# One tile and one move for queries and keys, the gate by tanh, and a new table of priorities in a three-part sequence mixer

## The chip, the cores and the metric

The kernel runs on one core of a Trainium2 chip. The metric is the time of one execution on the device in microseconds (us). Five engines work at the same time, each through its own queue and strictly in the order in which the program was written: TensorE (PE; its weight loads are shown as PEld), VectorE (DVE), ScalarE (ACT), GpSimd (POOL) and SyncE (SP), which here only issues DMA transfers. An engine that reaches an instruction whose inputs aren't there waits, and everything behind it in its queue waits too.

## What is computed

Four sequences of 768 steps with 8 heads of 48 channels (384 channels together) go through three parts.

```python
# 1. a linear recurrence per head, with complex decay
a = (a_re, a_im) * min(|a|, 0.999) / (|a| + 1e-6)
for t in range(S):
    S_re, S_im = a_re*S_re - a_im*S_im + outer(k[t], v[t]), a_re*S_im + a_im*S_re
    y[t] = q[t] @ S_re
x = y.reshape(B, S, 384)
# 2. a gate from a causal convolution of five taps
gate = 1 / (1 + exp(-conv(x, conv_w)));   x = (gate * (x @ w_val)) @ w_out
# 3. mixing over tokens
theta = x @ w_theta
u = x + w_tok_r @ (x * cos(theta)) + w_tok_i @ (x * sin(theta))
return u + max(u @ w_ch, 0)
```

## The kernel before

Each sequence is worked on in two halves of 384 steps, so there are eight halves `h`; channels lie on the 128 partitions in three blocks `m`. The stages of one half, by the names that the planner gives them:

- `pre_load`, `pre_a`, `pre_e`, `pre_u`, `pre_p` (function `half`): load decay, queries, keys and values; the logarithm of the decay's size and its running sum by a scan (ACT: Ln, Exp; DVE: products and scans), the running angle (ACT: Arctan, then Sin and Cos), and the products that turn `q` and `k` into four tiles, `qc`, `q` and `kc`, `k` (cosine and sine part of each). A square of the imaginary part (line 596) is always ACT's. The tiles `e`, `L`, `cc`, `kc`, `qc` are five allocations from one pool `xx` of three buffers.
- `pre_k`: transposes of `kc` and `k` on TensorE (line 679), copied into `ks`. `pre_m` (line 698): moves of the four tiles from channel layout into head layout, `KT` and `QT`, one pair of heads at a time. A head of 48 channels is one or two pieces of partitions, ten pieces for eight heads; four sources make 40 DMAs per half, 320 in all, from SP's queue.
- `att_s`, `att_q`, `att_x`, `att_m`: the running state, scores (line 746), their mask on DVE (line 750), the output, and its move back to channel layout `xT` (line 789).
- `gat_x`, `gat_c`, `gat_s`, `gat_v`, `gat_p` (function `gated`): split into two half-precision parts, the convolution (TensorE for the first two halves, DVE after, line 842), the gate by `Sigmoid` (lines 830 and 848), the value product times the gate, and the projection with its cosine and sine (lines 902 and 904).
- `mix_y`, `mix_o`, per sequence: the mixing over tokens (line 933, the largest group of matmuls), then the last product (line 964) and the store.
- `w_val`, `w_out`, `w_tok`, `w_ch`: loading and splitting the weights, 37 loads (line 434), taken up by DVE and ACT mostly in the first 250 us.

All of this is first recorded as steps and then put in order by `Plan.order`, a list scheduler: of the steps that are ready it takes the one of lowest score, where a score is a priority by stage and half (`TUNE["aim"]`), a slope within the stage, a price for an engine slower than the fastest that could do it (`slow`), and a price for a change of ACT's function table (`switch`). A step may have alternatives: a copy out of PSUM goes to ACT or DVE. ACT holds one set of functions at a time; a step that names its sets (`table=`) makes `emit` put a table load (line 225) ahead of it when the current set is none of them. Before, `Ln` and `Exp` are one set, `Sigmoid` and `Arctan` can share a second, `Sin` and `Arctan` a third. Flags of the values' ranges are collected in `flag` and summed at the end (line 1009); if one fails, a slow general path runs, which takes no part here.

Of the kernel before, what the change touches and what calls it, by code (L numbers as in the profile page):

```python
# [21 lines left out]
NC = 3  # L22
# [38 lines left out]
class Lazy:  # L61
# [15 lines left out]
class Plan:  # L77
# [37 lines left out]
    def touch(self, st, t):  # L115
        if t not in st.tiles:
            st.tiles.append(t)
            self.claim(t)
# [113 lines left out]
def STAGE(i):  # L232
# [5 lines left out]
    slow=7.561879865749755e+17, switch=6.288666508159823e+19,  # L238
    aim=dict(
        att_m=(2.6995250415312483e+20, -7.969025655037973e+20, 2.6228837826230804e+19, 2.6900520492997217e+20, -8.834881158532012e+18, -2.879741646661289e+20, -5.6941031593171996e+20, 2.3047449587628616e+18),  # L240
        att_q=(-3.098021878434935e+20, -1.1402659875657051e+20, 1.887862893900206e+20, -2.8577290015113812e+20, -1.4315973604769672e+20, 2.6812851596232865e+20, 2.72275845311613e+20, 7.860040540285524e+20),
        att_s=(-8.1055449031404e+20, -7.491206287610686e+20, 2.9358157753418138e+19, -3.8325095700157596e+20, -6.619979384008357e+20, -2.234011386790889e+20, -5.975838226088282e+20, 1.6686986873077983e+20),
        att_x=(1.1113433647480439e+19, -5.647427977795909e+20, -2.8460971411064858e+20, 5.586815476186121e+19, 1.2318998677514333e+20, 3.819798462611895e+20, 2.275797624242207e+20, 3.855677298476604e+20),
        gat_c=(-1.3939695215960621e+20, 8.573466356105659e+20, 2.2571713871496027e+20, 3.3867600113954475e+20, 5.5553098301983103e+20, 3.7001570014350914e+20, 2.5679529280869446e+20, 3.9509943083354974e+20),
        gat_p=(1.1079553435472739e+20, -5.8677250143246785e+20, -3.039805067631806e+20, 1.3995532506697353e+20, 1.4368282293569442e+19, -4.8003306508215596e+20, -5.888518038921008e+19, 3.3768391232254136e+20),
        gat_s=(-1.859713821331812e+20, -1.4068539620445092e+20, 1.2272979418679604e+20, 1.0910490888272282e+20, 1.975120382740974e+20, 2.7909999301427043e+20, -2.5984925365397773e+20, 3.503112540032319e+20),
        gat_v=(-8.243593242166855e+19, -4.8478023647103314e+20, 2.6272218123939388e+20, 7.870475005876767e+20, -2.922333136132161e+20, 2.180085968308735e+20, 8.681066273223144e+19, 6.446000807147153e+19),
        gat_x=(-3.817467868176136e+19, -5.5407993524252e+20, -2.3538641088770815e+20, -5.286011864109842e+19, 1.2214160515683628e+20, -4.3994221524293557e+20, -1.2611788232525521e+20, -8.341909703175887e+20),
        mix_o=(-2.8734628221397905e+19, -1.5117821435577077e+20, 5.5180557681850335e+19, -3.0992713400204735e+20, 8.898697985755559e+19, 1.7189691487411024e+19, 6.015575849622989e+19, 4.689053187148435e+20),
        mix_y=(1.8267901924410455e+20, 4.718088521769894e+18, 2.6659420514735283e+20, 3.8919266864908095e+20, 3.004006273230587e+20, 1.2053661079841625e+21, 2.7156940596173242e+20, 8.425222082850524e+20),  # L250
        pre_a=(-2.1563070898003165e+20, -1.3407216796584958e+20, 6.598887458043333e+20, 4.288137829766081e+20, 2.7732396744020797e+20, 3.7528707274748146e+20, 4.205374047444239e+20, -5.4573270371167496e+20),
        pre_e=(-7.88945782665487e+19, -2.41133541333048e+20, 3.56175050953755e+20, -2.2958653295810013e+20, 2.0580757847809894e+20, -4.06329427432926e+20, 1.4426176750414936e+19, 3.7503300425471115e+19),
        pre_k=(-3.8194358638246057e+18, -4.690711155477919e+20, -1.05651341434556e+20, -3.8497518485941315e+20, 4.801003520091643e+18, 8.729949699788487e+19, 3.3221443421105107e+19, 8.525573064665427e+19),
        pre_load=(1.3647208663803196e+20, 1.7155210766295656e+20, 3.2799160663234006e+20, 3.643770839616477e+20, -8.83912647730307e+20, 1.0804960952804722e+20, 5.5648036868185824e+20, 1.1333686388887786e+20),
        pre_m=(-1.0319521449344616e+20, 1.8639307935649297e+20, -1.96775082810374e+20, 2.582688938750491e+20, 5.142607771115187e+20, 2.687818958364026e+19, -3.5416465535944786e+20, 1.7837533526089567e+20),
        pre_p=(-1.3761746888669947e+20, 6.39581395858005e+20, 7.44612787205641e+20, 1.3673500528991615e+20, 1.579699019194403e+20, 3.6993958742260076e+20, -2.1781512347217582e+20, 3.930708276628839e+20),
        pre_u=(-5.860711647029067e+19, -3.402301592630338e+20, 1.7263712425624768e+20, 3.0143430377465636e+20, -7.724555404449633e+20, 2.7932201631581952e+20, -8.401409740176993e+19, 1.536761573530841e+18),
        w_ch=(9.679107120691147e+18, -8.567667523970695e+19, 9.84845351623264e+19, 2.0631282111325136e+20, 1.2792621986728021e+20, 1.2299703092890036e+20, 8.444280747653703e+19, 9.810840497961917e+19),
        w_out=(2.4173937984678797e+19, 1.8189247227344226e+19, 6.998474788081834e+19, 1.80638580129783e+20, 1.0592462196430992e+20, 1.0269092211592351e+20, 5.455113029523955e+19, 6.902520285647893e+19),
        w_tok=(-2.4274300307598315e+20, 8.890738857751473e+19, -6.164473229195098e+20, 4.051552711302278e+20, -1.5994422517121417e+20, 1.8111768451654405e+20, 1.133253904891538e+20, 9.650836120777289e+19),  # L260
        w_val=(1.885596508505931e+20, -5.177513586728041e+19, 1.3298879856064614e+18, 1.1360663686930627e+20, 2.738565137956907e+19, 2.9941767965625594e+19, 6.726488094765722e+18, -1.1531895753208386e+19)),
# [56 lines left out]
def fast_path(ctx: ExitStack, tc: tile.TileContext, ri, qk, v, w_val, conv_w, w_out, w_theta, w_tok, w_ch, out, count):  # L318
# [234 lines left out]
    def half(h):  # L553
# [6 lines left out]
        def both(ms):  # L560
# [6 lines left out]
            def put(alts, reads, writes, table=None, flag=()):  # L567
# [3 lines left out]
                for t in (*reads, *writes):  # L571
                    if isinstance(t, Lazy):
                        plan.touch(st, t)
# [700 lines left out]
```

## Time and profile before

| | us |
|---|---|
| median of three runs (552.32 to 554.35) | 553.67 |
| the profiled execution | 553.85 |
| its span, first to last instruction | 552.1 |
| TensorE busy in the span | 463.4 |
| VectorE busy | 451.6 |
| ScalarE busy, of it 54 table loads | 350.9, of it 69.3 |

The span is 1.75 us shorter than the execution's own time. A busy share is a mean over stages with different limits, so the table alone tells of no stage what holds it. TensorE's matmuls overlap and their ends are modelled; its busy time is no statement on its rate.

### The profile page before, as it was taken

To read this page: it belongs to the slowest core of one execution; us is meant where nothing else is said; L and a number is where in the kernel's file an instruction comes from. 1 tells how busy PE (TensorE), PEld (TensorE's weight loads), DVE (VectorE), ACT (ScalarE), POOL (GpSimd) and SP (SyncE) were. 2 spreads that over 40 slices of the span, in tenths; PEclk is the share of its full clock that TensorE was granted. 3 is DMA by queue.
4 is the path that set the end of the run, shared out by engine and by line. 5 is a ranking of instruction groups with operands and counts; after the bars stand their busy time and mean duration, and the time that the engine had idled before them with its cause. 6 is when DMAs were issued, how large, how long until landed. Compare 5 with 4: busy or idle time off the path is not lost.

```text
span 552.1 us, 10792 instructions
## 1 busy us (share of the span) xinstructions
PE 463.4 (84%) x4111; PEld 314.3 (57%) x4111; DVE 451.6 (82%) x792; ACT 350.9 (64%) x565; POOL 8.2 (1%) x32
## 2 busy tenths in 40 slices
PE   0026859868996779899999989999999999999993
PEld 0016646646674456666667666677677766655661
DVE  3799999799979898999999997999987573784222
ACT  6998968877948668886988786679563112521000
POOL 0000001000000000000000000000000000000000
PEclk9997976999997889999999999999999999999997
DMA  8847375654447445753125364242122200000001
GB/s 286 311 144 240 117 241 129 203 159 141 149 135 215 117 118 151 218 182 117 44 77 187 86 197 149 78 131 76 47 77 75 70 25 30 15 14 1 30 28 35
DMA packets 39563, 66.87 MB, mean 121 GB/s; under 512 B 8272, under 2 KB 31312, under 8 KB 39504
## 3 DMA queue, kind: packets, MB, share of 16 engines
q1 hardware_dynamic: 39504, 66.11, 38.9%
q8 instruction: 34, 0.56, 0.5%
q14 instruction: 25, 0.20, 0.1%
HBM read 37.76 MB, written 4.72 MB: 77 GB/s over the span
## 4 chain that ended last, share of the span: by engine, by line
PE 42%; DVE 22%; ACT 16%; DMA 10%; SPq 6%; issue 3%; DVEq 0%; ACTq 0%
PE mm L933 17%; PE mm L884 7%; SPq L698 5%; PE mm L964 5%; ACT L225 3%; DMA zt<-in_w_tok_dram 3%; PE sc L746 3%; PE mm L858 3%; PE x L763 3%; DMA xT<-xs 2%; DVE ri L645 2%; PE x L768 2%; DVE at L750 2%; DVE ri L365 2%; DVE g L842 2%
## 5 line engine op out<-in xcount | busy, mean ns | idle before, releaser
L933 PE MATMUL mm<-zz,wt_sb 128*128 128x384 f16 x864 | 147.0, 326 | 0.0
L933 PEld LDWEIGHTS <-wt_sb 128*128 128x128 f16 x864 | 84.3, 98 | 53.1 <-issue 0.6
L884 PE MATMUL mm<-wo_sb,gHL 128*128 128x384 f16 x432 | 79.3, 338 | 4.1 <-DVE zt L365 4.1
L225 ACT ACT_TABLE_LOAD x54 | 69.3, 1283 | 1.7 <-PEq L1261 0.8
L884 PEld LDWEIGHTS <-gHL 128*128 128x128 f16 x432 | 42.9, 101 | 33.3 <-issue 9.2
L746 PE MATMUL sc<-QT,KT 96*128 96x128 f32 x384 | 54.2, 291 | 6.1 <-DMA QT<-q 3.8
L746 PEld LDWEIGHTS sc<-QT,KT 96*128 96x128 f32 x384 | 50.4, 204 | 10.5 <-issue 3.3
L356 ACT ACTIVATE uHL<-tr 128x384 f16<-128x384 f32 x18 | 8.8, 486 | 63.9 <-PE tr L949 63.9
L679 PE MATMUL tr<-ident,xx 128*128 128x128 f32 x72 | 14.8, 315 | 40.6 <-DVE xx L362 34.8
L763 PE MATMUL x<-at,v 128*64 128x128 f32 x384 | 40.9, 289 | 8.1 <-DVE at L750 7.3
L858 PE MATMUL mm<-xHL,wv_sb 128*128 128x384 f16 x216 | 38.4, 326 | 3.4 <-ACT g L830 1.2
L842 DVE SCALAR_TENSOR_TENSOR g<-xT,cw_sb,g 128x384 f32<-128x384 f32 x72 | 40.9, 610 | 0.1
L964 PE MATMUL mm<-wc_sb,uHL 128*128 128x384 f16 x216 | 39.4, 326 | 1.8 <-ACT uHL L356 1.2
L763 PEld LDWEIGHTS x<-at,v 128*64 128x64 f32 x384 | 26.1, 140 | 16.8 <-issue 7.4
L768 PE MATMUL x<-QT,ws 96*48 96x128 f32 x320 | 35.4, 284 | 0.0
L679 PEld LDWEIGHTS tr<-ident,xx 128*128 128x128 f32 x72 | 9.2, 155 | 45.3 <-issue 29.8
L750 DVE TENSOR_TENSOR at<-sc,tri 128x384 f32<-128x384 f32 x64 | 33.7, 551 | 0.2
L858 PEld LDWEIGHTS <-wv_sb 128*128 128x128 f16 x216 | 20.7, 98 | 17.1 <-issue 4.7
L964 PEld LDWEIGHTS <-uHL 128*128 128x128 f16 x216 | 20.5, 98 | 16.4 <-ACT uHL L356 1.6
L365 DVE SCALAR_TENSOR_TENSOR u<-x,mm 128x384 f32<-128x384 f32 x24 | 13.2, 549 | 17.5 <-PE mm L933 17.3
L362 DVE TENSOR_TENSOR zt<-zt,x 128x768 f32<-128x768 f32 x24 | 22.9, 954 | 4.2 <-ACT zt L904 3.1
L365 DVE SCALAR_TENSOR_TENSOR r<-mm,u 128x384 f32<-128x384 f32 x24 | 13.2, 552 | 13.6 <-PE mm L964 13.3
(155 smaller groups left out, 831.1 us busy)
## 6 DMA issues: line engine op xcount, KB each, us to landing
ri<-in_ri_dram SPq DMA_DIRECT2D x14, 576.0 KB, 4.6
zt<-in_w_tok_dram SPq DMA_DIRECT2D x20, 384.0 KB, 3.8
v<-in_v_dram SPq DMA_DIRECT2D x8, 576.0 KB, 5.9
out_dram<-r SPq DMA_DIRECT2D x24, 192.0 KB, 2.0
q<-in_qk_dram SPq DMA_DIRECT2D x7, 576.0 KB, 5.7
k<-in_qk_dram SPq DMA_DIRECT2D x7, 576.0 KB, 5.6
KT<-xx SPq DMA_DIRECT2D x48, 72.0 KB, 2.2
KT<-k SPq DMA_DIRECT2D x48, 72.0 KB, 2.2
```

The lines of the kernel that those rows point to most:

```text
L225: load_table(table)
L365: return [dve(n, lambda: V.scalar_tensor_tensor(out=out(), in0=a(), scalar=scalar, in1=b(), op0=op0, op1=op1, **kw))]
L698: nc.sync.dma_start(out=o()[cs * D + d0:cs * D + d0 + n, i, :], in_=src()[p0:p0 + n, m, :])
L746: T.matmul(out=ps()[:, c, :], lhsT=kT()[:, i, cs], rhs=qT()[:, i, cs], start=(c == 0), stop=(c == NC - 1), skip_group_check=True)
L750: add([dve(HALF, lambda ps=ps, at=at: V.tensor_tensor(out=at(), in0=ps(), in1=tri.unsqueeze(1).to_broadcast([P, NC, P]), op=ALU.mult))], r ...
L763: T.matmul(out=x()[64 * i:64 * i + 64, cs], lhsT=vt()[:, c, hh * D:hh * D + 64], rhs=ats[i]()[:, c, :], start=(c == 0), stop=(c == NC - 1 ...
L768: T.matmul(out=x()[64 * i:64 * i + D, cs], lhsT=ws[c]()[:, hh * D:(hh + 1) * D], rhs=qT()[:, i, cs], start=False, stop=(c == NC - 1), skip ...
L842: add([dve(HALF, lambda m=m, t=t: V.scalar_tensor_tensor(out=g()[:, m], in0=xT()[:, m, t:t + HALF], scalar=cw_sb[:, m, t:t + 1], in1=g()[: ...
L858: T.matmul(out=ps(), lhsT=wv_sb[:, kk, a, m * P:(m + 1) * P], rhs=xHL()[:, b, kk, 4:], start=(kk == 0 and i == 0), stop=(kk == NK - 1 and ...
L884: T.matmul(out=ps(), lhsT=gT()[:, a, kk, c * P:(c + 1) * P], rhs=wo_sb[:, kk, j, b], start=(kk == 0 and i == 0), stop=(kk == NK - 1 and i ...
L933: T.matmul(out=y(), lhsT=wt_sb[:, j, r, a, s * P:(s + 1) * P], rhs=zz_t[b, s]()[:, e, r], start=(s == 0 and r == 0 and i == 0), stop=(s == ...
L964: T.matmul(out=pv(), lhsT=uHL()[:, a, kk], rhs=wc_sb[:, kk, e], start=(kk == 0 and i == 0), stop=(kk == NK - 1 and i == 2))
```

## The change

- The queries and keys of a half are loaded into one tile `qk`, and `e`/`cc`/`qc` and `L`/`kc` share the two parts of one tile `xx` (class `Part` names one part). One DMA then moves both the query's and the key's piece of a head, into one tile `QK`: 20 DMAs of twice the bytes per half in place of 40. A move now names both parts as its inputs. `xx` has two double buffers in place of three single ones, `qk` two double ones in place of two and two, `x2` six in place of seven.
- The gate is computed as tanh of half the argument; the product with the values becomes (gate + 1) times value, and the factor one half goes into the next scale. `Tanh` is asked for in a set that also holds `Sin`. Sets: `Sin` of the gate in the same set as `Tanh`, `Arctan` first in the set that holds `Sin`. A maximum over every eighth gate value goes into eight new flags per partition.
- The square of `pre_a` may go to DVE as well.
- The value tile's padding lies at its end alone, and its load has a stage of its own (`pre_v`).
- The whole table `TUNE` has other numbers; the prices `slow` and `switch` stand in another ratio to the priorities.

```diff
-SET_SIG = ("sigmoid_and_others",)
-SET_SIN = ("trig_and_small",)
-SET_ATAN = ("sigmoid_and_others", "trig_and_small")
+SET_TANH = ("silu_and_others", "sigmoid_and_others")
+SET_SIN = ("trig_and_small", "silu_and_others")
+SET_SIN2 = ("silu_and_others", "trig_and_small")
+SET_ATAN = ("trig_and_small", "sigmoid_and_others")
...
+class Part:
+    def __init__(self, whole, i):
+        self.whole, self.i = whole, i
+    def __call__(self):
+        return self.whole()[:, self.i]
...
-    slow=7.561879865749755e+17, switch=6.288666508159823e+19,
+    slow=5.041324337085933e+27, switch=1.2587493578880431e+20,
...
-        re, im, q, k = (lazy(t, [P, NK, HALF]) for t in ("ri", "ri", "q", "k"))
-        e, L, cc, kc, qc = (lazy("xx", [P, NK, HALF]) for _ in range(5))
+        re, im = (lazy("ri", [P, NK, HALF]) for _ in range(2))
+        qk_t, xx = lazy("qk", [P, 2, NK, HALF]), lazy("xx", [P, 2, NK, HALF])
+        q, k = Part(qk_t, 0), Part(qk_t, 1)
+        e = cc = qc = Part(xx, 0)
+        L = kc = Part(xx, 1)
...
-            put([act(n, lambda x=im_, y=e_: A.activation(out=y(), in_=x(), func=AF.Square))], [im], [e])
+            put([act(n, lambda x=im_, y=e_: A.activation(out=y(), in_=x(), func=AF.Square)),
+                 dve(n, lambda x=im_, y=e_: V.tensor_tensor(out=y(), in0=x(), in1=x(), op=ALU.mult))], [im], [e])
...
-            for nm, dst_t, parts in (("KT", KT_t, (kc, k)), ("QT", QT_t, (qc, q))):
-                                nc.sync.dma_start(out=o()[cs * D + d0:cs * D + d0 + n, i, :], in_=src()[p0:p0 + n, m, :])
+                for cs, (src, pair) in enumerate(((xx, (qc, kc)), (qk_t, (q, k)))):
+                            nc.sync.dma_start(out=o()[cs * D + d0:cs * D + d0 + n, :, i, :], in_=src()[p0:p0 + n, :, m, :])
+                        add([dma(8 * n * HALF, move, True)], reads=[(t, m) for t in pair], writes=[(o, i, cs, d0)])
...
-            add([act(n3, lambda: A.activation(out=g(), in_=g(), func=AF.Sigmoid))], reads=[g] + gm, writes=gm,
-                table=SET_SIG)
+            add([act(n3, lambda: A.activation(out=g(), in_=g(), func=AF.Tanh, scale=0.5))], reads=[g] + gm, writes=gm,
+                table=SET_TANH)
+        add([("dve", 150.0, lambda: V.tensor_reduce(column(F_GATE + h), g()[:, 0, ::8], axis=AX.X, op=ALU.max))],
+            reads=[(g, 0)], writes=[("flag", F_GATE + h)])
...
-            add(tt(ALU.mult, HALF, lambda m=m: g()[:, m], ps, lambda m=m: g()[:, m]), reads=[ps, (g, m)],
+            add(stt(HALF, lambda m=m: g()[:, m], lambda m=m: g()[:, m], 1.0, ps, ALU.add, ALU.mult), reads=[ps, (g, m)],
```

Three places in the built order show what moves. A row is one instruction, or several alike in a row; a tile's name is followed by what it is made from.

SP's queue, before, from the first moves of the second half (`KT` and `QT` from `xx`, `k` and `q`) on, with a load of token weights (L434) among them:

```order
L698 DMA KT<-xx 48x384 x2
L698 DMA KT<-xx 32x384
L698 DMA KT<-xx 16x384
L698 DMA KT<-k 48x384 x2
L698 DMA QT<-xx 48x384
L434 DMA zt<-in_w_tok_dram 128x768
L698 DMA QT<-xx 48x384
L698 DMA QT<-q 48x384 x2
L698 DMA KT<-k 32x384
L698 DMA KT<-k 16x384
L698 DMA KT<-xx 48x384
L698 DMA KT<-k 48x384
```

Six more rows of such moves follow there before the next load. SP's queue, after, at the same place (L807 is the move back to `xT`, L448 the load of token weights):

```order
L716 DMA QK<-xx 48x2x384 x2
L716 DMA QK<-xx 32x2x384
L716 DMA QK<-xx 16x2x384
L716 DMA QK<-xx 48x2x384
L807 DMA xT<-xs 48x384 x2
L716 DMA QK<-qk 48x2x384 x2
L716 DMA QK<-qk 32x2x384
L716 DMA QK<-qk 16x2x384
L716 DMA QK<-qk 48x2x384
L448 DMA zt<-in_w_tok_dram 128x768
```

The same two pairs of heads now take ten moves in place of twenty, and the next load of weights stands behind ten of them.

ACT's queue, before, at the program's start (the first half, by blocks of channels; L596 is the square):

```order
L591 ACTIVATE ri<-ri 128x384
L593 ACTIVATE xx,flag<-ri 128x384
L596 ACTIVATE xx<-ri 128x384
L598 ACTIVATE xx,flag<-xx,one 128x384
L601 ACTIVATE xx<-ri,lneps 128x384
L591 ACTIVATE ri<-ri 128x384
```

ACT's queue, after, at the same place (L609 and L611 are the Ln and Exp, L617 the second Ln):

```order
L609 ACTIVATE ri<-ri 128x384
L611 ACTIVATE xx,flag<-ri 128x384
L609 ACTIVATE ri<-ri 128x384
L611 ACTIVATE xx,flag<-ri 128x384
L617 ACTIVATE xx,flag<-xx,one 128x384 x2
L620 ACTIVATE xx<-ri,lneps 128x384
```

The square has left ACT's queue; DVE has it there (L615, `xx<-ri`), and two blocks go through each step before the next.

ACT's queue, before, where the sine of one half (L902, L904) meets the gate of the next (L848):

```order
L225 ACT_TABLE_LOAD
L902 ACTIVATE zt<-zt 128x384
L904 ACTIVATE zt<-zt,halfpi 128x384
L225 ACT_TABLE_LOAD
L848 ACTIVATE g<-g 128x1152
L356 ACTIVATE uHL<-tr 128x384
L225 ACT_TABLE_LOAD
L902 ACTIVATE zt<-zt 128x384
L904 ACTIVATE zt<-zt,halfpi 128x384
```

ACT's queue, after, where the same two meet (L924, L926 the sine, L866 the gate):

```order
L926 ACTIVATE zt<-zt,halfpi 128x384
L680 ACTIVATE xx<-xx,halfpi 128x1152
L370 ACTIVATE ws<-w 96x384
L370 ACTIVATE zz<-zt 128x768
L916 ACTIVATE zt<-mm 128x384
L866 ACTIVATE g<-g 128x1152
L370 ACTIVATE x_2862<-mm 128x384
L370 ACTIVATE uHL<-tr 128x384
L922 ACTIVATE zt<-zt 128x384
L924 ACTIVATE zt<-zt 128x384
```

No load stands between the gate and the sines around it. The built order of the fast path holds 39 table loads in place of 54, and 349 DMAs in place of 509.

## Rows read from the trace of the kernel before

**Rows 1.** Busy us of each engine (instructions) in five stretches; granted clock, DMA.

```profile
core 0: us, PE busy (x) PEld busy (x) DVE busy (x) ACT busy (x) POOL busy (x), PEclk, DMA share, GB/s
0.00:28.00 28.00, 0.00 (x0) 0.00 (x0) 16.71 (x39) 22.97 (x45) 2.35 (x12) 1.00 0.83 299
28.00:84.00 56.00, 32.85 (x326) 24.90 (x326) 56.00 (x113) 48.06 (x99) 0.30 (x2) 0.86 0.60 185
84.00:224.00 140.00, 117.56 (x1119) 81.27 (x1119) 124.74 (x208) 108.35 (x167) 3.31 (x9) 0.91 0.51 151
224.00:540.00 316.00, 310.04 (x2656) 206.81 (x2653) 250.90 (x422) 170.99 (x256) 2.19 (x10) 1.00 0.28 84
540.00:552.10 12.10, 2.93 (x18) 1.35 (x16) 3.21 (x14) 0.49 (x1) 0.00 (x0) 0.75 0.12 40
```

**Rows 2.** The chain that ended last, shares of the span by engine.

```profile
PE 42%; DVE 22%; ACT 16%; DMA 10%; SPq 6%; issue 3%; DVEq 0%; ACTq 0%
```

**Rows 3.** DVE's waits from 84 to 224 us: for whom, us, times, longest.

```profile
DVE zt L439 <- DMA zt<-in_w_tok_dram: 4.2, 2, 3.7
DVE x L358 <- PE mm L884: 1.6, 2, 0.9
DVE ri L608 <- ACT xx L601: 1.6, 1, 1.6
DVE zt L439 <- DMA zt<-in_w_ch_dram: 1.2, 1, 1.2
DVE g L362 <- ACT g L848: 1.0, 1, 1.0
...
DVE wt_sb L365 <- ACT wt_sb L407: 0.2, 1, 0.2
```

**Rows 4.** DVE's waits in the first 28 us, the longest.

```profile
DVE ri L362 <- ACT xx L593: 5.0, 3, 3.4
```

**Rows 5.** DMA issues of line 698 on SP: duration ns least/median/most, first and last start.

```profile
L698 SPq DMA_DIRECT2D QT<-q x80: 503/589/1750, 34.7 to 432.0; - x80
```

**Rows 6.** SP's timeline, 79 to 97 us: start, us, what.

```profile
79.72 2.41 SPq L698 DMA_DIRECT2D KT<-xx  x4
...
94.36 1.15 SPq L581 DMA_DIRECT2D ri<-in_ri_dram  x1
95.62 0.84 SPq L434 DMA_DIRECT2D zt<-in_w_tok_dram  x2
```

**Rows 7.** DMA issues: count, size, median us from issue to landing.

```profile
out_dram<-r SPq DMA_DIRECT2D x24, 192.0 KB, 2.0
...
KT<-xx SPq DMA_DIRECT2D x48, 72.0 KB, 2.2
```

**Rows 8.** ACT's timeline around a table load: start, us, what.

```profile
96.02 1.16 ACT L606 ACTIVATE ri<-ri 128x1152 f32<-128x1152 f32 x1
97.20 1.28 ACT L225 ACT_TABLE_LOAD   x1
98.50 0.49 ACT L830 ACTIVATE g<-mm 128x384 f32<-128x384 f32 x1
```

**Rows 9.** Groups by line and shape: busy us, mean ns, idle before.

```profile
L225 ACT ACT_TABLE_LOAD x54 | 69.3, 1283 | 1.7 <-PEq L1261 0.8
...
L362 DVE TENSOR_TENSOR ri<-ri,xx 128x1152 f32<-128x1152 f32 x7 | 9.5, 1352 | 0.0
...
L660 ACT ACTIVATE ri<-ri 128x1152 f32<-128x1152 f32 x7 | 8.1, 1158 | 0.0
...
L848 ACT ACTIVATE g<-g 128x1152 f32<-128x1152 f32 x6 | 7.0, 1163 | 2.8 <-DVE g L842 2.7
...
L398 DVE TENSOR_REDUCE flag<-gHL 128x1 f32<-128x48 f16 x4 | 0.9, 223 | 0.0
```

**Rows 10.** DVE's timeline, back to back work: start, us, what.

```profile
93.27 0.55 DVE L365 SCALAR_TENSOR_TENSOR zt<-zt 128x384 int32<-128x384 int32 x1
93.73 0.54 DVE L365 SCALAR_TENSOR_TENSOR wt_sb<-zt,wt_sb 128x384 f16<-128x384 f32 x1
```

More of the change, by code (lines that the diff above doesn't have):

```diff
@@ L115, in touch @@
     def touch(self, st, t):
+        t = t.whole if isinstance(t, Part) else t
         if t not in st.tiles:
@@ L302 @@
         pre_a=0.0,
-        pre_e=0.0,
-        pre_u=6145.339050871748))
+        pre_e=13729.237869499897,
+        pre_u=2123.5850288312477))
 def segments(h):
@@ L568, in put @@
                 plan.sub = ms[0]
-                st = add(alts, reads=[x for t in reads for x in (names(t) if isinstance(t, Lazy) else [t])],
+                st = add(alts, reads=[x for t in reads for x in (names(t) if isinstance(t, (Lazy, Part)) else [t])],
                          writes=[x for t in writes for x in names(t)] + list(flag), table=table)
                 for t in (*reads, *writes):
-                    if isinstance(t, Lazy):
+                    if isinstance(t, (Lazy, Part)):
                         plan.touch(st, t)
@@ L727, in state @@
                     for at in range(0, 2 * D, 32):
-                        T.matmul(out=w()[at:at + 32, o], lhsT=rows[:, at:at + 32], rhs=vt()[:, c, o],
+                        T.matmul(out=w()[at:at + 32, o], lhsT=rows[:, at:at + 32], rhs=vt()[:, c * CH + hh * D:c * CH + (hh + 1) * D],
                                  start=(ti == 0 and hh == 0), stop=(hh == H - 1), skip_group_check=True)
@@ L745, in score @@
                     cs = slice(c * P, (c + 1) * P)
-                    T.matmul(out=ps()[:, c, :], lhsT=kT()[:, i, cs], rhs=qT()[:, i, cs], start=(c == 0),
+                    T.matmul(out=ps()[:, c, :], lhsT=qk_()[:, 1, i, cs], rhs=qk_()[:, 0, i, cs], start=(c == 0),
                              stop=(c == NC - 1), skip_group_check=True)
-            add([pe(654, score, 0.75)], reads=[qT, kT] + parts(qT) + parts(kT), writes=[ps])
+            add([pe(654, score, 0.75)], reads=[qk_] + parts(qk_), writes=[ps])
             add([dve(HALF, lambda ps=ps, at=at: V.tensor_tensor(
@@ L762, in attend @@
                     hh = 2 * p + i
-                    T.matmul(out=x()[64 * i:64 * i + 64, cs], lhsT=vt()[:, c, hh * D:hh * D + 64], rhs=ats[i]()[:, c, :],
+                    T.matmul(out=x()[64 * i:64 * i + 64, cs], lhsT=vt()[:, c * CH + hh * D:c * CH + hh * D + 64], rhs=ats[i]()[:, c, :],
                              start=(c == 0), stop=(c == NC - 1 and ws[c] is None), skip_group_check=True)
@@ L767, in attend @@
                         hh = 2 * p + i
-                        T.matmul(out=x()[64 * i:64 * i + D, cs], lhsT=ws[c]()[:, hh * D:(hh + 1) * D], rhs=qT()[:, i, cs],
+                        T.matmul(out=x()[64 * i:64 * i + D, cs], lhsT=ws[c]()[:, hh * D:(hh + 1) * D], rhs=qk_()[:, 0, i, cs],
                                  start=False, stop=(c == NC - 1), skip_group_check=True)
@@ L772, in heads @@
         add([pe(128 * 2 * (3 + n_ws), attend, 0.77)],
-            reads=ats + [vt, (vt, "pad"), qT] + parts(qT) + [w for w in ws if w is not None], writes=[x])
+            reads=ats + [vt, (vt, "pad"), qk_] + parts(qk_) + [w for w in ws if w is not None], writes=[x])
         add(copy(HALF, lambda: xs()[:64 + D], lambda: x()[:64 + D]), reads=[x], writes=[xs])
@@ L829, in gated @@
             plan.touch(plan.steps[-1], g)
-            add([act(HALF, lambda m=m, ps=ps: A.activation(out=g()[:, m], in_=ps(), func=AF.Sigmoid, scale=1.0 / (SX * SW)), psum=True)],
-                reads=[ps], writes=[(g, m)], table=SET_SIG)
+            add([act(HALF, lambda m=m, ps=ps: A.activation(out=g()[:, m], in_=ps(), func=AF.Tanh, scale=0.5 / (SX * SW)), psum=True)],
+                reads=[ps], writes=[(g, m)], table=SET_TANH)
             plan.touch(plan.steps[-1], g)
```

160 lines of the change are left out of this document (82 added, 78 removed).

## The prediction

> **What bounds the kernel now.** I read the stretches first [rows 1]. From 224 to 540 us TensorE is busy for 310.0 of 316 us at a granted clock of 1.00: there the end is set by TensorE's work and by nothing else. Before that it isn't: TensorE starts late and is busy for 32.9 of 56 and 117.6 of 140 us. In those stretches DVE is the fullest engine: 56.0 of 56 us, then 124.7 of 140. So the kernel runs behind DVE until TensorE has work enough, and behind TensorE from then on. What sets the time is how early DVE has released TensorE's work, and how long DVE stood still on the way: 28 - 16.7 = 11.3 us in the first 28, none to 84, 140 - 124.7 = 15.3 us to 224.
>
> The chain of waits [rows 2] gives TensorE 42%, DVE 22%, ACT 16%, DMA 10% and SP's issuing 6%. ACT and SP aren't full, but they stand between two pieces of DVE's work. DVE's waits from 84 to 224 us [rows 3] show where: two kinds of wait for a load of weights (4.2 and 1.2, together 5.4 us), eleven rows of waits for ACT, from 1.6 down to 0.2, together 6.9 us, and three for TensorE (the first 1.6).
>
> For the order I used one measure: at a matmul, the DVE work that the order puts ahead of what this matmul needs, plus TensorE's work from it to the end. No time can be below that sum. I took each instruction at its row's median time to the engine's next start, because the recorded ends overlap: 0.46 us between two starts where the record says 0.55 [rows 10]; for TensorE at the lower quartile, its full-clock pace. Over all rows that makes 441 us of DVE, 350 of ACT, 429 of TensorE. Before, the highest sum is 307.3 + 197.9 = 505.2 us, in the attention of the sixth half, and the sums are over 500 from the fourth half on. ACT's lead at the start adds to it: there ACT's rows ahead of DVE's exceed DVE's own by 6.6 us, which makes 511.8. With DVE's other idle time ahead of 224 us (4.7 + 15.3), TensorE's 6.0 idle us from 224 to 540 and the 12.1 - 2.9 = 9.2 at the end [rows 1] that is 547.0 of the span's 552.1; 5.1 us stay unplaced. So the measure is close enough to read a change by.
>
> **The change, part by part.** *Order and moved work.* The built order has 15 ACT loads less (15 x 1.283 = 19.2 us [rows 9]); in exchange more copies out of PSUM stand on ACT, so ACT sums to 336 us, 14 less, and DVE to 438, 3 less. In the last figure are squares that DVE takes over (two of 1.35 us [rows 9] and three small ones) and the eight new maxima (8 x 0.22 = 1.8 us [rows 9]). The highest DVE sum is now 259.3 + 248.9 = 508.2 us, at the first mixing product of the second sequence, 3.0 above before. But the start is better balanced: with the squares gone from ACT its lead is 2.3 us in place of 6.6, and both together make 510.5 against 511.8. Term: **-1.3 us**, from +3.0 (if the start doesn't matter) to -4.3.
>
> *The merged moves.* 320 issues of 0.589 us [rows 5] are 188 us of SP's queue; 160 go, so 94 us at the same price. A move has twice the runs, and if its issue cost twice, nothing would be saved; issues of 16, 32 and 48 partitions lie in the same narrow median, so I take the same price. Landing: 72 KB take 2.2 us, 192 KB 2.0 [rows 7], so 144 KB cost nothing more; the scores behind them don't wait longer. What the issues cost before is visible once: from 79.72 us SP issues moves until 94, and only then, at 95.62, the next two loads of weights [rows 6]; DVE's longest wait for a load, 3.7 us, is for one of them [rows 3]. In the new order ten moves stand at that place, not twenty. Of the 5.4 us I take half: **-2.7**, from 0 (the load waits for its buffer, not for the queue) to -5.4. A merged move waits for query and key both; behind it in SP's queue stand moves to `xT` and loads of weights, for which TensorE's gate and DVE would wait. The key's product is the earlier one and the scores need both, so I count that at zero; its price, if a load is held by one more product of 1.35 us [rows 9], is in the slower rival.
>
> *Table loads.* Ahead of that mixing product there stand 28 loads in place of 37. Nine of 37 are a quarter, so I take a quarter of DVE's 6.9 us behind ACT: **-1.7**, from 0 to -6.9. After 224 us the rest of ACT's saving is hidden by TensorE. The row prices a switch at the load alone: 97.20 + 1.28 = 98.48, and the next activation starts at 98.50; the one before ended at 97.18 [rows 8]. The Trainium skill, page "ScalarE: Activation LUTs", section "What ACT_TABLE_LOAD costs", gives the same 1283 ns but adds a drain of about 1380, 2.66 us for a switch. By that the 15 loads would be 39.9 us, an estimate, this term would double and the time would be 545.7; the trace shows no such gap.
>
> *Start.* The first half's value load, 576 KB or 1.9 us at 299 GB/s [rows 1], stood between the loads of the first and second block and now stands behind all. DVE's waits there are 5.0 us in three, of which 3.4 is the first landing [rows 4]; the other 1.6 can shrink. **-0.8**, from 0 to -1.6.
>
> *At zero.* Tanh for Sigmoid: functions of one shape take the same time (1163 and 1158 ns [rows 9]). The added one in the gate's product rides in an instruction of the same shape. Six `x2` in place of seven: the six `zz` are held by the same steps and stay six, so they cover it; without that cover a projection would wait for the mixing of the sequence before. Two double `xx`: the new order lets the third half's first stage begin after 79 us of DVE's work, before after 89, so they hold nothing back there. One more comparison of flags at the end, **+0.2**, bounded by the small reduction's 0.22 [rows 9].
>
> Sum: -1.3 - 2.7 - 1.7 - 0.8 + 0.2 = -6.3. The profiled execution took 553.85 us and lies 0.2 above the median; against the median, 553.7 - 6.3 = **547.4 us**.
>
> **The rivals.** *DVE's new order decides (slower).* The waits are set by where the order puts a need, and a new order may wait as long as the old. Then the sum of 508.2 against 505.2 is what counts, at the first mixing product of the second sequence: 553.7 + 3.0 + 0.2 = 556.9. It decides if DVE has by then again stood still for about 26.6 us (11.3 + 15.3). For it: the new order's sums are over 500 from 146 us of DVE's work on, the old one's from 178, so TensorE's supply is short from an earlier point and any stall after it counts; one held load by a merged move adds 1.35. Against it: 14 us less ACT work and 160 fewer issues are around DVE.
>
> *Saved beside the path (no change).* ACT and SP have idle time already; their saving makes more of it, and DVE's waits, which are mostly for one product just asked for, stay. Only order and flag count: 553.7 - 1.3 + 0.2 = 552.6. For it: ACT is busy for 108 of 140 us to 224 [rows 1], not full. Against it: it is a queue in order, where a load in front delays the one result that DVE needs.
>
> *All of it (much faster).* All waits of DVE for loads and for ACT from 84 us on and the start's 1.6 go: 553.7 - 1.3 - 5.4 - 6.9 - 1.6 + 0.2 = 538.7. Against it: some of these waits are TensorE's turn-around at one remove.
>
> **How the numbers follow.** The forecast, 543 to 551, has 0.45; all of it 0.13; no change 0.24; slower 0.18. A measurement of this kernel can tell about 0.5% from no change, which is 550.9 to 556.4. So faster 0.58, same 0.24, slower 0.18. The range reaches from just above the full gain to the slower rival: 540 to 557.
>
> **What would show it.** Right: DVE's idle time before 84 us falls from 11.3 towards 6; its waits for `in_w_tok` and `in_w_ch` fall to some 2.7; 39 loads on ACT; 160 moves of about 0.6 us on SP; TensorE is full from about 218 us on. The slower rival shows as DVE idle for 15 us or more between 84 and 224, and TensorE idle before the second sequence's mixing. Wrong altogether: an issue of a merged move that takes over 1 us, or TensorE idle for clearly more than 6 us after it has once been full.

## The result and the profile after

The changed kernel takes **534.46 us** (median of 4 runs, 533.23 to 535.73) beside 554.01 for the kernel before on the same chip (552.32 to 554.85): a ratio of 0.9651, 95% interval 0.9618 to 0.9684, 19.5 us less. The sign was forecast; the time is 13 us below the forecast and 5.5 below the range.

The profiled execution took 533.23 us, its span is 531.4. The stretches of after, in the columns of [rows 1]; the last two are cut at 520, where after's full phase ends:

```profile
0.00:28.00 28.00, 0.00 (x0) 0.00 (x0) 20.68 (x54) 23.28 (x47) 2.31 (x12) 1.00 0.87 313
28.00:84.00 56.00, 38.63 (x326) 29.38 (x326) 56.00 (x107) 49.12 (x95) 0.68 (x2) 0.88 0.63 186
84.00:224.00 140.00, 123.38 (x1241) 86.14 (x1241) 137.46 (x228) 115.84 (x184) 1.72 (x9) 0.98 0.60 169
224.00:520.00 296.00, 293.84 (x2536) 197.39 (x2533) 227.90 (x399) 147.85 (x232) 4.53 (x9) 1.00 0.28 79
520.00:531.40 11.40, 2.12 (x13) 0.80 (x11) 3.11 (x15) 0.49 (x1) 0.00 (x0) 0.76 0.12 42
```

DVE, the engine that the kernel runs behind until 224 us, is now busy for 137.5 of 140 us where it was for 124.7, and it does 228 instructions there in place of 208. Its idle time is 28 - 20.68 = 7.3 us at the start (11.3 before) and 2.5 us from 84 to 224 (15.3 before). DVE's longest waits from 84 to 224 us, to be laid beside [rows 3], and its longest in the first 28 us, beside [rows 4] and two more rows of before (the last two):

```profile
DVE zt L453 <- DMA zt<-in_w_tok_dram: 0.7, 1, 0.7
DVE zt L917 <- PE mm L906: 0.5, 1, 0.5
DVE g L379 <- PE mm L880: 0.3, 1, 0.3
DVE zt L455 <- ACT zt L451: 0.3, 1, 0.3
...
DVE ri L376 <- ACT xx L611: 5.2, 2, 3.4
...
DVE ri L608 <- ACT xx L601: 1.7, 2, 1.0
DVE ri L365 <- ACT xx L598: 1.3, 1, 1.3
```

The chain of waits, beside [rows 2]: what is left of it belongs to the two engines that are full. DMA, ACT and SP's issuing held 32% of it and now hold 12.

```profile
PE 54%; DVE 29%; ACT 7%; DMA 4%; issue 3%; SPq 1%; DVEq 0%; ACTq 0%
```

The saved work itself: the merged moves' issues (duration least/median/most, as [rows 5]), their landing (as [rows 7]) and ACT's table loads (as [rows 9]):

```profile
L716 SPq DMA_DIRECT2D QK<-xx x80: 583/607/1417, 29.8 to 409.7; - x80
L716 SPq DMA_DIRECT2D QK<-qk x80: 583/602/1054, 33.5 to 410.3; - x80
...
QK<-xx SPq DMA_DIRECT2D x48, 144.0 KB, 3.0
QK<-qk SPq DMA_DIRECT2D x48, 144.0 KB, 3.1
...
L237 ACT ACT_TABLE_LOAD x39 | 50.0, 1283 | 1.5 <-PEq L1284 0.8
```

**Where the 20.7 us of span went.** Cut the span at 224 us. It is then DVE's busy and idle time ahead of the cut plus TensorE's busy and idle time behind it. Before: 197.45 + 26.6 + 313.0 + 15.1 = 552.1. After: 214.14 + 9.9 + 296.0 + 11.4 = 531.4. The two busy terms together are 510.4 and 510.1. So only 0.3 us of the gain is work that went away on the engine that bounds: the rest is standing still that went away, 4.0 us of DVE at the start, 12.7 of DVE from 84 to 224, 3.7 of TensorE behind. TensorE's busy time in all fell too, from 463.4 to 458.0 us, at a granted clock of 0.98 in place of 0.91 from 84 to 224 us; but that is ahead of the cut, where DVE sets the pace. Two experiments below speak against the clock as a cause: e8 had 0.79 from 28 to 84 us and 0.96 from 84 on and took the time of after (0.88 and 0.98), and e10 had 0.97 and 0.95 and took the time of before (0.86 and 0.91).

### The profile page after: what moved, and what is told of

It is laid out like the page before. It is cut to its first block, busy times and chain, and to the rows that moved or that the text cites. A ratio compares the mean times of both kernels' runs of the same rounds, so it can differ in the third digit from the quotient of the medians.

```text
span 531.4 us, 10524 instructions
## 1 busy us (share of the span) xinstructions
PE 458.0 (86%) x4111; PEld 313.7 (59%) x4111; DVE 445.2 (84%) x797; ACT 336.6 (63%) x555; POOL 9.2 (2%) x32
## 4 chain that ended last, share of the span: by engine, by line
PE 54%; DVE 29%; ACT 7%; DMA 4%; issue 3%; SPq 1%; DVEq 0%; ACTq 0%
PE mm L955 21%; PE mm L906 10%; PE mm L986 6%; PE mm L880 4%; PE sc L764 4%; DVE qk L376 3%; PE x L781 3%; PE x L786 2%; DVE zt L455 2%; DVE ri L664 2%; DVE at L768 2%; DVE zt L379 2%; ACT L237 2%; PE tr L698 1%; DVE xx L376 1%
## 5 line engine op out<-in xcount | busy, mean ns | idle before, releaser
L906 PE MATMUL mm<-wo_sb,gHL 128*128 128x384 f16 x432 | 75.6, 329 | 0.1
L764 PE MATMUL sc<-QK 96*128 96x128 f32 x384 | 55.7, 295 | 6.8 <-DVE at L768 5.0
L764 PEld LDWEIGHTS sc<-QK 96*128 96x128 f32 x384 | 51.3, 207 | 10.3 <-DVE at L768 5.7
L370 ACT ACTIVATE uHL<-tr 128x384 f16<-128x384 f32 x21 | 10.2, 486 | 72.3 <-PE tr L971 72.3
L781 PE MATMUL x<-at,v 128*64 128x128 f32 x384 | 39.7, 294 | 8.3 <-ACT xs L370 6.2
L698 PE MATMUL tr<-ident,xx 128*128 128x128 f32 x72 | 14.4, 308 | 34.2 <-DVE xx L376 31.2
L768 DVE TENSOR_TENSOR at<-sc,tri 128x384 f32<-128x384 f32 x64 | 34.5, 549 | 1.5 <-PE x L781 1.2
L781 PEld LDWEIGHTS x<-at,v 128*64 128x64 f32 x384 | 24.7, 144 | 16.7 <-ACT xs L370 7.0
L786 PE MATMUL x<-QK,ws 96*48 96x128 f32 x320 | 33.7, 283 | 0.0
L376 DVE TENSOR_TENSOR qk<-qk,ri 128x1152 f32<-128x1152 f32 (+1 forms) x30 | 33.0, 1110 | 0.5 <-ACT ri L650 0.5
L986 PEld LDWEIGHTS <-uHL 128*128 128x128 f16 x216 | 20.7, 98 | 15.0 <-DVE uHL L379 1.2
L880 PEld LDWEIGHTS <-wv_sb 128*128 128x128 f16 x216 | 20.8, 98 | 13.7 <-issue 1.3
```

Source lines behind the costliest of these rows:

```text
L376: return [dve(n, lambda: V.tensor_tensor(out=out(), in0=a(), in1=b(), op=op))]
L698: T.transpose(ps()[:, m, :], src()[:, m, c * P:(c + 1) * P], ident)
L764: T.matmul(out=ps()[:, c, :], lhsT=qk_()[:, 1, i, cs], rhs=qk_()[:, 0, i, cs], start=(c == 0), stop=(c == NC - 1), skip_group_check=True)
L768: add([dve(HALF, lambda ps=ps, at=at: V.tensor_tensor(out=at(), in0=ps(), in1=tri.unsqueeze(1).to_broadcast([P, NC, P]), op=ALU.mult))], r ...
L781: T.matmul(out=x()[64 * i:64 * i + 64, cs], lhsT=vt()[:, c * CH + hh * D:c * CH + hh * D + 64], rhs=ats[i]()[:, c, :], start=(c == 0), sto ...
L786: T.matmul(out=x()[64 * i:64 * i + D, cs], lhsT=ws[c]()[:, hh * D:(hh + 1) * D], rhs=qk_()[:, 0, i, cs], start=False, stop=(c == NC - 1), ...
```

## The experiments

Unless said otherwise, an experiment keeps the built order of its kernel word for word, as a list in place of the table of priorities, and changes only the part named. The list is shorter than the table, so line numbers are 80 to 90 smaller (the move is line 716 of after, 633 or 634 here). Two theories were put up: **A**, the saved issues and table loads took DVE's waits away; **B**, the new order did, and the saved work lies in idle time. In e7 and e10 the set of each table load is chosen by looking ahead along the fixed order. All ratios are to the kernel before, run on the same chip in the same session; differences between experiments of different sessions are less sure, since the median of before itself moved from 552.8 to 554.2 us.

This table has all twelve. "DVE idle" is ahead of the cut at 224 us, at the start and from 84 on; "PE idle" is behind it; "busy" is DVE's busy time ahead plus TensorE's behind. DVE's waits from 84 to 224 us are summed over all their rows by what ended them. These columns come from the one profiled execution of each kernel, whose time is within 2.4 us of the median (in e2, e4 and e11 3.0 to 7.4 us below it), so steps of 1 or 2 us in them say little. In e2, e3 and e11 DVE also stands still for 1.8 to 3.3 us from 28 to 84, which the table leaves out.

| kernel | median us | ratio (95%) | DVE idle 0-28 | 84-224 | PE idle | busy | waits for DMA / ACT / PE |
|---|---|---|---|---|---|---|---|
| before | 552.8 to 554.2 | 1 | 11.3 | 15.3 | 15.1 | 510.4 | 5.4 / 6.9 / 2.1 |
| e7, before + new table sets | 552.43 | 0.997 (0.994-0.999) | 12.2 | 13.7 | 14.4 | 509.2 | 5.4 / 7.0 / 0.5 |
| e6, before + second queue | 552.34 | 0.997 (0.994-0.999) | 11.5 | 11.2 | 15.9 | 510.3 | 1.4 / 8.4 / 0.2 |
| e10, before + both | 552.52 | 1.002 (0.998-1.005) | 11.8 | 10.2 | 17.1 | 510.1 | 1.9 / 7.4 / 0 |
| e9, new order, neither saving | 544.24 | 0.984 (0.978-0.990) | 7.6 | 7.6 | 14.1 | 510.9 | 0 / 6.1 / 1.0 |
| e1, after with 52 table loads | 542.76 | 0.979 (0.975-0.983) | 7.8 | 7.9 | 13.7 | 510.9 | 0.4 / 5.8 / 1.3 |
| e5, after, moves cut, two queues | 539.42 | 0.973 (0.969-0.977) | 7.8 | 5.0 | 12.8 | 510.8 | 0.3 / 1.0 / 3.4 |
| e12, after, half on POOL | 539.14 | 0.974 (0.967-0.980) | 7.3 | 7.1 | 13.6 | 510.1 | 0.5 / 0.2 / 6.2 |
| e8, after, squares on ACT | 534.95 | 0.966 (0.962-0.970) | 9.4 | 4.8 | 11.2 | 507.8 | 0.3 / 0.2 / 3.9 |
| after | 534.46 | 0.965 (0.962-0.968) | 7.3 | 2.5 | 11.4 | 510.1 | 0.7 / 0.7 / 0.8 |
| e2, after, moves cut, one queue | 594.57 | 1.075 (1.070-1.079) | 7.6 | 22.6 | 32.2 | 524.7 | 8.0 / 5.9 / 8.5 |
| e3, e1 and e2 and e8 together | 599.59 | 1.081 (1.076-1.086) | 9.9 | 26.0 | 34.5 | 523.7 | 11.2 / 7.7 / 7.0 |
| e4, new parts, old priorities | 625.53 | 1.129 (1.125-1.133) | 11.1 | 5.9 | 49.4 | 554.4 | 0.5 / 3.2 / 1.2 |
| e11, old parts, new priorities | 618.59 | 1.119 (1.111-1.127) | 10.8 | 19.5 | 43.0 | 534.3 | 5.5 / 5.6 / 7.8 |

### The table loads in the new order (e1)

```diff
-SET_TANH = ("silu_and_others", "sigmoid_and_others")
-SET_SIN = ("trig_and_small", "silu_and_others")
+SET_TANH = ("sigmoid_and_others",)
+SET_SIN = ("trig_and_small",)
-    func=AF.Tanh, scale=0.5 / (SX * SW)
+    func=AF.Sigmoid, scale=1.0 / (SX * SW)
```

> The changed kernel with its built order of steps kept as it is, but the gate computed by Sigmoid in its own set and the sets of before: 52 table loads in place of 39, 13 x 1.283 = 16.7 us more on ACT. Theory A (the saved work itself took DVE's waits away): DVE's waits for ACT come back towards the 6.9 us of before, time 540 to 543. Theory B (the new order of the steps took them away, the saved loads lie in ACT's idle time): no more than 2 us, 534 to 537.

Measured: 542.76 us, 8.3 more than after, for 13 loads of 1.283 us: half of ACT's 16.7 us comes through. DVE's waits for ACT are back (5.8 us; after had 0.7), and they are single waits for a result asked for just before:

```profile
DVE xx L293 <- ACT xx L597: 2.0, 1, 2.0
DVE zt L296 <- ACT zt L375: 1.8, 3, 1.0
DVE flag L786 <- ACT g L783: 1.1, 1, 1.1
```

So in the new order the loads matter much more than the 1.7 us that I gave them. By the two ratios (0.9789 and 0.9651) the price is 7.6 us rather than 8.3.

### The merged moves in the new order (e2, e3, e5)

e2 cuts each merged move in two again, on the same queue; e5 does the same and gives the queries' half to POOL's queue. e3 is e1, e2 and e8 (below) together.

```diff
-nc.sync.dma_start(out=o()[..., :, i, :], in_=src()[p0:p0 + n, :, m, :])
+for j in (1, 0):
+    nc.sync.dma_start(out=o()[..., j, i, :], in_=src()[p0:p0 + n, j, m, :])      # e2, e3
+    (nc.sync, nc.gpsimd)[1 - j].dma_start(...)                                   # e5
```

> The changed kernel, its order kept, but each merged move issued as two DMAs one behind the other, key then query: 509 DMAs in place of 349, 160 x 0.59 = 94 us more of SP's queue. Theory A: DVE's waits for weight loads come back from 0.7 towards 5.4 us and TensorE waits for scores, time 539 to 544. Theory B: no more than 2 us, 534 to 537.

> The changed kernel, its order kept, with both of the above and the five squares that DVE took back on ACT (5.0 us): the work of before in the order of after. Theory A: most of the 19.5 us gain goes, time 548 or more. Theory B: most of it stays, time 540 or less.

> The changed kernel in its own order, with each merged move cut in two again as in the run of the split moves, but the second half (the queries' 160) issued by POOL, whose engine had 8.2 us of work in the kernel before. Theory of the queue (the 60 us came from SP, which issues all transfers one behind the other and reaches the later ones late): SP's issue time goes back to about that of the changed kernel, PE's wait sc<-DMA QK<-qk of 27.3 us falls below 6, and the time comes back to 535 to 550 us. Rival, theory of the transfers (twice as many transfers, half as large, land late whoever issues them): the time stays at 580 to 600 us and the waits stay. Second rival: POOL's issues are slower than SP's, and the wait for QK moves to them: 550 to 580 us.

Measured: 594.57, 599.59 and 539.42 us. Cutting the moves costs 60 us, three times the whole gain; with the second half on another queue the kernel is 5 us slower than after. The work is the same and the number of transfers is the same: what costs is SP's queue, in which everything stands in order. In e2 TensorE waits 17 times for the queries and keys (first row), SP issues 16 moves one behind the other, from 134.58 to 145.5 us, with no load among them (the next rows: SP's timeline), and yet a move of 72 KB lands sooner after its issue, at the median, than a merged one of 144 KB does (the last row):

```profile
PE sc L682 <- DMA QK<-qk: 27.3, 17, 3.4
...
132.61 0.53 SPq L365 DMA_DIRECT2D zt<-in_w_tok_dram  x1
134.21 0.34 SPq L519 DMA_DIRECT2D v<-in_v_dram  x1
134.58 2.69 SPq L634 DMA_DIRECT2D QK<-qk  x4
137.37 3.02 SPq L634 DMA_DIRECT2D QK<-xx  x4
140.44 2.49 SPq L634 DMA_DIRECT2D QK<-qk  x4
142.98 1.22 SPq L634 DMA_DIRECT2D QK<-xx  x2
144.25 1.22 SPq L634 DMA_DIRECT2D QK<-qk  x2
145.51 0.58 SPq L515 DMA_DIRECT2D ri<-in_ri_dram  x1
...
QK<-qk SPq DMA_DIRECT2D x96, 72.0 KB, 2.2
```

In e5 that wait is 1.3 us. Neither A nor B in its pure form stands, and e2's time lies far outside both of its ranges: the parts matter in the new order, yet undoing them costs 65 us, which cannot be what they had gained. The new order is made for 160 moves and breaks with 320 on one queue. The 5 us of e5 are not shown to be the price of the cut: e12 (below) leaves the moves whole, gives half of them to POOL's queue as well and takes the same time, 539.14 us.

### The parts in the old order (e6, e7, e10)

e6 is the kernel before with the queries' 160 moves on POOL, which takes as many issues from SP as the merge does. e7 is the kernel before with the tanh and the new sets. e10 is both.

```diff
-nc.sync.dma_start(out=o()[cs * D + d0:cs * D + d0 + n, i, :], in_=src()[p0:p0 + n, m, :])
+(nc.sync if nm == "KT" else nc.gpsimd).dma_start(...)                 # e6, e10
-SET_SIG = ("sigmoid_and_others",)
-SET_SIN = ("trig_and_small",)
+SET_SIG = ("silu_and_others", "sigmoid_and_others")                   # e7, e10, with Tanh
+SET_SIN = ("trig_and_small", "silu_and_others")
```

> The kernel before in its own order, with the queries' 160 moves issued by POOL in place of SP; nothing else differs, so the sums of work on PE, DVE and ACT stay. Theory of the queue: in the kernel before, too, SP's issues held the loads of weights back; DVE's waits for w_tok and w_ch between 84 and 224 us, 5.4 us, fall below 2, PE's wait sc<-DMA QT<-q of 3.8 us falls, and the time is 543 to 550 us. Rival (the waits for loads in the kernel before came from where its order puts the loads, and SP's queue has room): 552 to 556 us with the waits where they were. A slower issue on POOL would show as PE's wait for QT above 3.8 us and a time above 556 us.

> The kernel before in its own order, with the gate from tanh in the sine's set and the sets' choice that follows, 49 table loads in place of 54; the moves and the flags stay as they were. Theory of the parts: a load is worth 0.64 us, as in the run with the sigmoid (8.3 us for 13 loads), so 5 loads give 3.2 us: 550.0 to 551.5 us. Theory of the order: without an order made for the new sets they give nothing, 553 to 555 us.

> The kernel before in its own order with both savings at once: the tanh sets (49 table loads) and the queries' 160 moves issued by POOL. Each alone gave 1.8 to 1.9 us. If they add up: 549.5 to 551.5 us, so the old order turns at most a fifth of the 19.5 us into time whatever is saved beside it. Rival (one hides behind the other, and both together free DVE): 540 to 547 us. Second rival (they cover the same wait): 552 us.

Measured: 552.34, 552.43 and 552.52 us beside 554.19 and, for e10, 552.76. One alone is at the edge of what can be told (0.997), both together are nothing that can be told (1.002, with an interval from 0.998 to 1.005). In its profile e6 does what its theory says for the waits, DVE's wait for loads falls from 5.4 us to 1.4, but its time is the rival's, and a good part of the fall never becomes time: waits for ACT grow from 6.9 to 8.4 us and TensorE's idle time behind the cut by 0.7. In e10 DVE stands still 5.0 us less from 84 to 224, and TensorE 2.0 more after. POOL's later landing, which shows in e12, isn't what eats the gain here: TensorE's waits for `QT` are 0.4 us in e6 and 1.5 in e10, 4.1 before. The merge itself was not tried in the old order.

Why the sets give next to nothing there is seen from where ACT's table loads stand. ACT's time in them (count) from 84 to 224 us and from 224 on: before, e10, e1, after, two rows each.

```profile
84.00:224.00 140.00, 25.08 (x20) 0.91 0.51 151
224.00:552.00 328.00, 30.79 (x24) 0.99 0.27 82
...
84.00:224.00 140.00, 25.62 (x20) 0.95 0.55 163
224.00:552.00 328.00, 24.38 (x19) 0.98 0.26 77
...
84.00:224.00 140.00, 28.23 (x22) 0.95 0.57 164
224.00:552.00 328.00, 26.94 (x21) 0.99 0.27 76
...
84.00:224.00 140.00, 21.78 (x17) 0.98 0.60 169
224.00:552.00 328.00, 16.71 (x14) 0.99 0.26 73
```

In the old order the sets save five loads, all of them after 224 us, where TensorE is the fuller engine (20 stay 20, 24 become 19). In the new order they save 13, five of them in DVE's stretch (22 become 17).

### The new order without the savings (e9)

Both edits above on after's order: Sigmoid with 52 loads, 320 single moves on two queues.

> The changed kernel's own order with neither saving in it: the gate by the sigmoid again (52 table loads) and 320 single moves, 160 of them issued by POOL so that SP's queue is no denser than in the changed kernel. What is left against the kernel before is the new order itself. If the two prices add up, 8.3 us for the loads and 5.0 for the divided moves: 546 to 549 us, so that the order alone is worth some 6 us of the 19.5 and the two savings in it some 13. Theory of the order alone: 535 to 542 us. Theory of the savings alone: 552 to 556 us, no better than the kernel before.

Measured: 544.24 us, 0.9837 (0.9777 to 0.9898), somewhat below what the two single prices add up to. Its stretches to 224 us:

```profile
0.00:28.00 28.00, 0.00 (x0) 0.00 (x0) 20.43 (x53) 23.03 (x47) 2.30 (x12) 1.00 0.86 310
28.00:84.00 56.00, 39.79 (x325) 30.14 (x326) 56.00 (x108) 49.07 (x94) 15.19 (x27) 0.88 0.61 186
84.00:224.00 140.00, 119.79 (x1199) 82.85 (x1199) 132.45 (x217) 118.76 (x182) 32.70 (x66) 0.96 0.56 164
```

The order alone, with room on the queue, is worth some 8.5 us (the interval of the ratio leaves 5.6 to 12.3). It brings the start from 11.3 us of idle time to 7.6, the squares on DVE included, and DVE's later idle time from 15.3 to 7.6. DVE no longer waits for a load at all; what is left, 6.1 us, is waits for ACT. Those are what the saved table loads then take (e1 against after), and the two savings in this order give 544.24 - 534.46 = 9.8 us. In the old order savings of the same kinds, though fewer loads, give nothing that can be told.

Two things limit this price list. e9 has a second queue, which before has not; beside e6, which has it too, the order is worth 0.9965 - 0.9837, or 7 us. And the second queue isn't free in the new order: e12 puts 4.7 us on it with all savings in place, so up to half of the 9.8 us can be the return of the moves to SP and not a saving, and then the order by itself is worth more than 8.5. So A against B comes out as both: the order is worth about 7 us or more, the savings in it 5 to 10, each with some 3 us of uncertainty from the intervals; the table loads are the part that a run shows singly (e1, 7.6 to 8.3).

### The squares, and the queue of the changed kernel (e8, e12)

e8 lets the square run on ACT only. e12 keeps the merged moves whole and issues the 80 of `qk` from POOL.

```diff
-put([act(n, ... Square), dve(n, ... ALU.mult)], [im], [e])
+put([act(n, ... Square)], [im], [e])                                  # e8
-nc.sync.dma_start(...)
+(nc.sync, nc.gpsimd)[cs].dma_start(...)                               # e12
```

> The changed kernel in its own order, with the 5 squares that its order gave to DVE put back on ACT, as in the kernel before; all else is the changed kernel. Theory of the start: DVE waited 7.3 us in the first 28 us of the changed kernel and 11.3 before, and the squares on DVE are what took the difference, so 3 to 5 us come back: 537 to 540 us. Rival: the squares lie beside other work, and DVE's saved time pays for ACT's: 533 to 536 us.

> The changed kernel in its own order with the 80 merged moves of queries and keys themselves (the other 80 are of their scaled parts) issued by POOL in place of SP, each still whole. If SP's queue still holds the changed kernel back, whose DVE waited 0.7 us for one load between 84 and 224 us and PE 0.8 us for QK: 530 to 533 us. If the merged moves have left room in it: 533 to 536 us. If POOL's issue makes the moves late: 536 to 541 us.

e8: 534.95 us, within the runs of after and the rival's case. DVE waits 2.0 us longer at the start and 2.2 later, and has 2.3 us less work in the sum; TensorE has 0.3 us less idle time. At the start DVE is busy for 18.64 us in place of 20.68: what it waits longer it has less to do. So the squares on DVE turn half of the 4.0 us of waiting into work and gain no time that can be told; the other half of the better start is the order's.

e12: 539.14 us, 4.7 slower than after (by the ratios too), the last of its three cases. SP's queue has room in the changed kernel, and the moves from POOL come later: they land 3.8 us after their issue (first row), TensorE waits for them, and DVE for the scores (TensorE's and DVE's waits from 84 to 224 us).

```profile
QK<-qk POOLq DMA_DIRECT2D x48, 144.0 KB, 3.8
...
PE sc L681 <- DMA QK<-qk: 4.1, 3, 2.5
...
DVE at L685 <- PE sc L681: 5.5, 3, 2.3
```

### The priorities exchanged (e4, e11)

Here the planner makes its own order: e4 is the changed code with the old table of priorities (the old `pre_load` row also for the new stage `pre_v`), e11 the old code with the new table.

> The changed kernel's parts with the priorities of before (the value load takes those of the other loads): the scheduler builds another order, with 37 table loads and 349 DMAs. Theory A: most of the gain is here too, 535 to 541. Theory B: most of it is gone, 548 to 560.

> The code of the kernel before with the new table of priorities, from which the planner makes an order of its own (57 table loads, two single moves in place of a merged one); the opposite corner to the new parts under the old priorities, 625.5 us. If the new priorities are better by themselves: 540 to 552 us. If a table of priorities is worth something only with the parts it was made for: above 570 us, with PE or DVE waiting tens of us at a few places.

Measured: 625.53 and 618.59 us (611.18 to 621.15). Both are far slower than either kernel, e4 outside both of its ranges, and that although it has the merged moves and only 37 table loads, two less than after. TensorE's longest wait in e4, then in e11, is one and the same, ahead of a transpose:

```profile
PE tr L490 <- DVE x L380: 35.3, 1, 35.3
...
PE tr L477 <- DVE x L367: 34.8, 1, 34.8
```

In these two cases a table of priorities is worth something only with the steps for which it was made. "The new priorities" therefore have no price by themselves; only the built order has one.

## Why the prediction was wrong

Laid out by the cut at 224 us, the forecast's -6.3 us and the span's -20.7 differ as follows.

- **What bounds the kernel** was read rightly: DVE until TensorE has work enough, TensorE from then on, and the time given by how long each stands still. Every kernel with a built order and room on the queue has 508 to 511 us of busy time in the table above. None of the signs of "wrong altogether" appeared: an issue of a merged move takes 0.61 us, and TensorE stands still for 2.2 us from 224 to 520.
- **The shares of DVE's waits: the step that failed.** From [rows 3] I took half of the 5.4 us for loads, and a quarter of the 6.9 behind ACT, because a quarter of the table loads ahead of that point went. Measured, 4.7 of 5.4 and 6.2 of 6.9 went; with TensorE's share DVE's idle time from 84 to 224 us fell by 12.7 us where the two terms had 4.4. That is 8.3 us of the miss. Here the waits did not shrink in proportion to the work of the engine waited for: between e1 and after five of 22 table loads in that stretch go, and 5.1 of DVE's 5.8 us of waits for ACT go with them. The forecast also gave the waits for loads to the merge alone and the order no part in them. A second queue takes 4.0 of the 5.4 us in the old order (e6), and with the new order all of them, without the merge (e9).
- **The order's term.** The highest sum of DVE's work ahead and TensorE's behind rose by 3.0 us, and I charged it. It was not paid: the busy time at the cut is 510.4 and 510.1 us. My sum bounds the time from below, and the kernel before stood 5.1 us above everything that I had placed on it; the new sum went into that room (in the same measure after closes at 508.2 + 7.3 + 2.5 + 2.2 + 9.3 = 529.5 of 531.4). 3.3 us of the miss.
- **TensorE's idle time behind the cut** had no term. It fell by 3.7 us. Of its waits there, those for DVE fell from 5.3 to 4.1 us, for moves from 1.5 to nothing, for ACT from 1.2 to 0.6; in e10, with the old order relieved, the idle time rose to 17.1. Why it fell with the new order was not taken apart.
- **The start.** ACT's lead was to fall by 4.3 us and DVE's waits for the first loads by 0.8, together 5.1; DVE's idle time in the first 28 us fell by 4.0. The size is nearly right, the parts aren't. The wait of [rows 4] is 5.2 us after and 5.0 before, so the later value load gave nothing. What went are waits behind ACT's later steps, as forecast: the two rows of 1.7 and 1.3 us shown above. But only half of it comes with the squares, which DVE then has to do itself (e8), and putting them back costs no time that can be told.
- **The merged moves' issue** costs 0.60 to 0.61 us at the median where I had 0.59: right. **Their landing** was to cost nothing more: 144 KB land after 3.0 to 3.1 us, 72 KB after 2.2 [rows 7]. The row of 192 KB in 2.0 us, a store of whole rows, was the wrong neighbour. It did little harm: TensorE waits 0.8 us for `QK` in after.
- **The price of a table load** on ACT was read rightly: 13 of them are 16.7 us. By the drain of 1380 ns that the Trainium skill adds (page "ScalarE: Activation LUTs", section "What ACT_TABLE_LOAD costs") they would be 34.6 us, an estimate. The trace shows no such drain: the next activation follows a load at once [rows 8], and ACT's busy time in e1 is 353.25 us against 336.58 after, 16.7 more. How much of the load ends up in the time is another question, and only the order answers it: half of it in e1, at most a little in e7 (five loads less, 0.997).

8.3 + 3.3 + 3.7 less 1.1 at the start is 14.2; with the flag's 0.2, which the cut doesn't show singly, that is the difference of 14.4.

**The rivals.** The slower one, the new sum without any relief, would have had to show 15 us or more of idle DVE; it shows 2.5. "No change, saved beside the path" is what happens to savings of these kinds in the old order (e10) and is wrong in the new. "All of it" was right on DVE's waits, though not on the order's part in them, and was still 4.2 us too slow, for want of TensorE's idle time and with the 3.0 us charged. I gave it 0.13; its argument against, that some waits are TensorE's turn-around at one remove, isn't borne out: DVE waits 0.8 us for TensorE in after, and in e10 not at all.

**What stays open.** Which steps of the new order give its 8.5 us was not taken apart, and what of it is the second queue's isn't known; the stretches place 3.7 us of idle time at the start and 7.7 from 84 to 224. The single prices (8.3 and 5.0) add up to 3.5 us more than both together (9.8), about as much as the interval of e9 leaves open (3.3 us to either side), so whether the two overlap isn't settled either. Nor is what the merge is worth where the queue has room: cut and whole moves on two queues take the same time (e5 and e12).

## What to carry to other kernels

Cut the span where the bounding engine changes, and write it as busy plus idle on each side: if the busy sum stays, the whole effect of a change is idle time on those engines, and each experiment can be read in that one row. Where a change comes with an order made anew, price a saving in the order that is built, by counting what goes ahead of the cut: five table loads saved behind it gave next to nothing, while thirteen, five of them ahead of it, took most of a wait. Here the waits for results that came just too late went nearly whole, so the case "all of it" deserved more than 0.13; no run took the work away in steps, so how such a wait goes in between isn't shown.

## What the runs showed of the hardware

- SP's issues are the price of a small move: 0.58 to 0.59 us each at the median for 24 to 72 KB (before), 0.60 to 0.61 for 48 to 144 KB (after). In e2 the durations of all of SP's issues add up to 289 of 590 us, and this queue, idle for half of the time, still cost 60 us; with half of the moves on POOL's queue the same order and the same transfers cost 5 (e5). In the old order, before, the issues add up to as much, 293 of 552 us, and relieving the queue brought 1.8 us (e6). So it is not the sum of the issues but where they stand in the queue.
- A merged move issued by POOL takes 0.59 us of POOL in the mean (80 moves of 48 to 144 KB in e12). One of 144 KB lands 3.8 us after its issue, one issued by SP in the same kernel after 3.2.
- Landing grows with size for these moves from partition to partition where SP alone issues: 2.2 us for 72 KB, 3.0 for 144. With two queues issuing, 72 KB take 2.6 to 3.3 us from either queue in the new order (e5, e9).
